# Second MLP in groups of 1024 tokens with seven block products per 2x2 product, the weight sums streamed from memory

## The chip, the cores and the metric

The kernel runs on one core of one Trainium2 chip. The metric is the device time of one execution in microseconds (us). TensorE (PE) multiplies, VectorE (DVE), ScalarE (ACT) and GpSimd (POOL) work on tiles elementwise, and SyncE (SP) issues the transfers between memory and the core's buffers (SBUF). TensorE adds its products up in eight banks of 128x512 float32 (PSUM).

## What is computed

An attention stage yields x, in 8 sequences of 576 tokens with 512 features; two MLP stages follow, the second of which the change touches:

```python
def _moe_ref(x, w_ch1, w_ch2):           # first MLP
    u = x + np.real(fft(fft(x, axis=1), axis=2))
    un = (u - mu) / np.sqrt(var + 1e-06)
    ch = np.maximum(un @ w_ch1, 0.0) @ w_ch2
    return u + ch

def _moe2_ref(x, U, V, w_ch1, w_ch2):    # second MLP
    h = x.transpose(0, 2, 1) @ U @ V
    u = x + h.transpose(0, 2, 1)
    ch = np.maximum(u @ w_ch1, 0.0) @ w_ch2
    return u + ch
```

In both MLPs w_ch1 is 512x2048 and w_ch2 2048x512. All of it is float32, 4608 tokens in all.

## The kernel before

Each MLP runs over NB = 9 blocks of BT = 512 tokens, and in each block over NF = 16 slices of 128 hidden features: 144 passes n for the first MLP (blocks 0 to 8) and 144 for the second (blocks 9 to 17). One loop emits them all. Matrix products take the format fp32r, in which a float32 number is split into a rounded high part and a low part (the difference). Each product is made of three: low times high, high times low, high times high, added up in one bank.

A pass n does the following. `split_w2` and `split_w1` (for two passes ahead) split the slices of the weights: ScalarE rounds (L185, L193), GpSimd or VectorE subtracts (L186, L194). `emit_l1` multiplies the slice of layer one with the block's inputs `xh`, `xl`, 12 products of 128x512 (L208 to L210) into a bank `h`; ScalarE takes relu and rounds into `gh` (L213), VectorE makes the low part `gl` (L214). `emit_l2` of the pass before then adds 12 products into four banks `acc` (L228 to L230 in the first MLP, L232 to L234 in the second). So TensorE has 24 products in a pass, and 384 in a block. After a block's last pass `finish_b` adds u from `t_xsum` (GpSimd, L674) to the four banks and stores the result (L680, L681).

Beside the passes, the table `side[n]` lists what is emitted after pass n: tasks of attention, and `prep_b(j)` for the second MLP, which loads tokens (`t_x2`, L612), splits them (`t_xs`, L625), projects them with U into `pt` (`t_pt`, L635, ten products per sequence) and builds the inputs in transposed form, tile `u` in the trace (`t_u2`, L661 with V, four transposes at L664; then `xh`, `xl`, L666 and L667). The weights of the second MLP are converted during the first by `w_pre` and kept in memory in `wb_d`; `w_get` loads them during block 8. The pool `wpool` then holds all 32 tiles of 128x512.

Order: no scheduler moves anything (`manual_schedule`); on each engine the instructions stand as the code emits them, and each queue, SP's with the transfers too, works strictly in that order. An instruction that waits holds up all behind it on its engine.

## Time and profile before

| | |
|---|---|
| median of 3 runs | 1880.99 us (1880.36 to 1881.33) |
| span of the profiled execution | 1881.6 us; its time outside the profiler is not listed apart |
| TensorE, products / weight loads | busy 1803.6 / 1502.3 us |
| VectorE, ScalarE, GpSimd | busy 953.9, 760.9, 682.0 us |
| second MLP | from 1049.8 us on, some 92.5 us a block |

The profile lists one execution on the chip: the busy time of each engine, groups of equal instructions by line (L12 is line 12 of the kernel), what released an idle engine, and the chain of work that ended last. Products overlap in the records: one of 128x512 is marked busy for some 0.39 us, although the next starts sooner, so the distance of the starts tells the rate. PEld are the weight loads that go with each product.

### The profile page before, as it was taken

How to read it: one execution, taken by the hardware profiler on the slowest of the kernel's cores; microseconds unless marked ns; L12 is line 12 of the kernel's file. 1: busy time of each engine (PE TensorE's matmuls, PEld its weight loads, DVE VectorE, ACT ScalarE, POOL GpSimd, SP SyncE). 2: the span in 40 equal slices, each digit the busy share in tenths (PEclk: the TensorE clock that was granted, in tenths of full speed). 3: DMA queues.
4: the chain of work that ended last, by engine and by line, in shares of the span. 5: the costliest groups of instructions: out<-in, count | busy, mean ns of one | idle time of the engine just before them, and what ended most of it. 6: DMA issues, size and time to landing. Idle time of an engine off the chain costs nothing.

```text
span 1881.6 us, 22636 instructions
## 1 busy us (share of the span) xinstructions
PE 1803.6 (96%) x8520; PEld 1502.3 (80%) x8520; DVE 953.9 (51%) x1494; ACT 760.9 (40%) x1448; POOL 682.0 (36%) x544
## 2 busy tenths in 40 slices
PE   5679999999999999999999999999999999999998
PEld 4557778788887878878888888888888888888887
DVE  6688865858677585845343333333333333333232
ACT  4565343434444343433443333334434343333332
POOL 2456444454534445442222222222222223232322
PEclk8889999999999999999999999999999999999999
DMA  6635324251432425003133101010101010100000
GB/s 249 235 104 205 123 96 147 74 180 57 147 129 97 146 77 177 34 26 86 56 124 111 63 0 51 1 45 1 51 1 45 1 51 1 45 1 23 1 23 23
DMA packets 61517, 146.16 MB, mean 78 GB/s; under 512 B 11144, under 2 KB 13720, under 8 KB 58400
## 3 DMA queue, kind: packets, MB, share of 16 engines
q1 hardware_dynamic: 61408, 144.72, 22.1%
q8 instruction: 67, 1.10, 0.3%
q14 instruction: 42, 0.34, 0.1%
HBM read 106.91 MB, written 39.43 MB: 78 GB/s over the span
## 4 chain that ended last, share of the span: by engine, by line
PE 80%; DVE 11%; ACT 3%; DMA 2%; POOL 1%; issue 1%; SPq 0%; POOLq 0%; ACTq 0%; DVEq 0%
PE h L208 12%; PE h L210 12%; PE h L209 12%; PE acc L234 7%; PE acc L232 7%; PE acc L233 7%; PE acc L228 5%; PE acc L230 5%; PE acc L229 5%; DVE f L333 2%; DMA raw<-in_w2a 2%; DVE eh L362 1%; PE o L294 1%; PE kv L273 1%; DVE f L328 1%
## 5 line engine op out<-in xcount | busy, mean ns | idle before, releaser
L186 POOL TENSOR_TENSOR w1l<-w,w1h 128x512 fp32r<-128x512 f32 x276 | 360.4, 1306 | 959.4 <-ACT w1h L185 959.3
L214 DVE SCALAR_TENSOR_TENSOR gl<-h,gh 128x512 fp32r<-128x512 f32 x288 | 198.3, 689 | 396.7 <-ACT gh L213 396.5
L213 ACT ACTIVATE gh<-h 128x512 fp32r<-128x512 f32 x288 | 171.7, 596 | 500.3 <-PE h L210 498.1
L194 DVE TENSOR_TENSOR w2l<-w,w2h 128x512 fp32r<-128x512 f32 x272 | 214.7, 789 | 179.3 <-ACT w2h L193 178.6
L228 PE MATMUL acc<-w2h,gl 128*128 128x512 f32 x576 | 231.9, 403 | 29.4 <-DVE gl L214 29.2
L193 ACT ACTIVATE w2h<-w 128x512 fp32r<-128x512 f32 x288 | 180.8, 628 | 159.8 <-PE acc L234 111.5
L229 PE MATMUL acc<-w2l,gh 128*128 128x512 f32 x576 | 229.6, 399 | 8.2 <-POOL w2l L194 8.2
L208 PE MATMUL h<-xl,w1h 128*128 128x512 f32 x576 | 228.5, 397 | 1.4 <-DVE xl L531 1.4
L230 PE MATMUL acc<-w2h,gh 128*128 128x512 f32 x576 | 228.9, 397 | 0.0
L208 PE MATMUL h<-xlb,w1h 128*128 128x512 f32 x576 | 227.5, 395 | 0.0
L210 PE MATMUL h<-xhb,w1l 128*128 128x512 f32 x576 | 225.3, 391 | 0.0
L210 PE MATMUL h<-xh,w1l 128*128 128x512 f32 x576 | 225.2, 391 | 0.0
L209 PE MATMUL h<-xh,w1h 128*128 128x512 f32 x576 | 225.1, 391 | 0.0
L209 PE MATMUL h<-xhb,w1h 128*128 128x512 f32 x576 | 224.9, 390 | 0.0
L234 PE MATMUL acc<-gh,w2h 128*128 128x512 f32 x576 | 224.8, 390 | 0.0
L232 PE MATMUL acc<-gh,w2l 128*128 128x512 f32 x576 | 224.2, 389 | 0.0
L233 PE MATMUL acc<-gl,w2h 128*128 128x512 f32 x576 | 224.1, 389 | 0.0
L185 ACT ACTIVATE w1h<-w 128x512 fp32r<-128x512 f32 x288 | 179.9, 625 | 15.1 <-DVE w L116 15.1
L228 PEld LDWEIGHTS acc<-w2h,gl 128*128 128x128 f32 x576 | 110.3, 192 | 59.8 <-DVE gl L214 34.5
L229 PEld LDWEIGHTS acc<-w2l,gh 128*128 128x128 f32 x576 | 110.5, 192 | 33.0 <-POOL w2l L194 10.9
L230 PEld LDWEIGHTS acc<-w2h,gh 128*128 128x128 f32 x576 | 110.8, 192 | 23.4
L210 PEld LDWEIGHTS h<-xh,w1l 128*128 128x128 f32 x576 | 108.3, 188 | 23.9
(137 smaller groups left out, 2642.3 us busy)
## 6 DMA issues: line engine op xcount, KB each, us to landing
kv<-in_kvm SPq DMA_DIRECT2D x14, 1280.0 KB, 9.5
q<-in_qT SPq DMA_DIRECT2D x8, 1220.0 KB, 9.2
x_d<-x2o SPq DMA_DIRECT2D x36, 256.0 KB, 2.1
x2f<-x_d SPq DMA_DIRECT2D x36, 256.0 KB, 4.2
outT<-o SPq DMA_DIRECT2D x36, 256.0 KB, 2.1
u_d<-x SPq DMA_DIRECT2D x32, 256.0 KB, 2.4
raw<-in_w1b SPq DMA_DIRECT2D x16, 512.0 KB
raw<-in_w2b SPq DMA_DIRECT2D x16, 512.0 KB, 4.7
```

Of the source, the lines that this page charges most:

```text
L186: (nc.vector if n in on_dve else nc.gpsimd).tensor_tensor(out=al, in0=a, in1=f32(ah), op=ALU.subtract)
L194: (nc.gpsimd if n in CLP else nc.vector).tensor_tensor(out=cl, in0=c, in1=f32(ch), op=ALU.subtract)
L208: nc.tensor.matmul(out=h, lhsT=ah[:, kc, :], rhs=xl[:, kc, :], start=(kc == 0), stop=False)
L209: nc.tensor.matmul(out=h, lhsT=ah[:, kc, :], rhs=xh[:, kc, :], start=False, stop=False)
L210: nc.tensor.matmul(out=h, lhsT=al[:, kc, :], rhs=xh[:, kc, :], start=False, stop=(kc == 3))
L214: nc.vector.scalar_tensor_tensor(out=gl, in0=h, scalar=0.0, in1=f32(gh), op0=ALU.max, op1=ALU.subtract)
L228: nc.tensor.matmul(out=a, lhsT=gl[:, tt], rhs=ch, start=s, stop=False)
L229: nc.tensor.matmul(out=a, lhsT=gh[:, tt], rhs=cl, start=False, stop=False)
L230: nc.tensor.matmul(out=a, lhsT=gh[:, tt], rhs=ch, start=False, stop=e)
L232: nc.tensor.matmul(out=a, lhsT=cl[:, tt], rhs=gh, start=s, stop=False)
L233: nc.tensor.matmul(out=a, lhsT=ch[:, tt], rhs=gl, start=False, stop=False)
L234: nc.tensor.matmul(out=a, lhsT=ch[:, tt], rhs=gh, start=False, stop=e)
```

## The change

Block 0 of the second MLP (passes 144 to 159) stays. The other eight blocks become four groups of two blocks, `group(1)` to `group(4)`, after the loop. In a group each layer is a product of matrices cut into 2x2 blocks, with seven block products in place of eight by the Strassen-Winograd scheme: four sums of blocks on the side of the weights, four on the side of the inputs, and sums of the products afterwards.

- **Units.** A layer has 56 units, seven products p for each of eight row blocks (m in layer one, i in layer two), of six matrix products of 128x512 each. `P1` runs skewed over m, so that products of neighbouring m alternate; `P2` runs one p over all i. Layer one stands wholly ahead of layer two, its results `G[m]`, four tiles of 128x512, in the buffers that held the weights.
- **Layer one.** Products 0, 4, 5 and 2 of an m add up in one bank `y`, 3 and 6 in `zz`, 1 in `z` (an `h` bank). After each product `post1` copies or adds the partial sum out, on ScalarE or VectorE.
- **Layer two.** `make` splits the input of each unit five units (`LEAD`) ahead, a rounding on ScalarE and a subtraction on VectorE, into six buffers. `plan` spreads over the units the sums T1, T2, T4 of `G`, the output sums F (`o_add`) and, for the next group, the input sums S, roundings H and low parts L (`x_sum`, `x_hi`, `x_lo`). `t_u2` of the next group runs in units 1 to 8 and stores u in memory (`ub_d`); `o_load` loads it again for the output.
- **Weights.** The seven weight blocks of each row block, split into high and low part, are made once by 16 `job`s in four steps a pass apart, two passes from job to job, and stored in `wv_d` (2 x 56 tiles of 256 KB). In the groups `v_load` streams them back, 512 KB for two units, four pairs ahead, into five buffers `v`.
- `split_w1`, `split_w2` and GpSimd have no work in the groups.

```diff
+    def u_copy(j, dc, ps):
+        half, k = divmod(dc, 2)
+        q = (0, 1, 5, 6)[half if j % 2 else 2 + half]
...
+        nc.scalar.activation(out=xb[q, k], in_=ps, func=AF.Copy)
+        nc.sync.dma_start(out=ub_d[j - 1][128 * dc:128 * dc + 128, :], in_=xb[q, k])
...
+    def x_tmp(q, k):
+        xb[q, k], where = x2_tile(f"xb{q}_{k}")
+        x2_held.append(where)
+    def x_sum(p, k):
+        b11, b21, t3, b22 = (xb[q, k] for q in (0, 1, 5, 6))
+        if p == 5:
+            nc.vector.tensor_tensor(out=t3, in0=b22, in1=t3, op=ALU.subtract)
+            return
+        if p == 2:
+            xb[2, k] = b21
+        else:
+            x_tmp(p, k)
+        if p == 4:
+            nc.vector.tensor_tensor(out=xb[4, k], in0=t3, in1=b11, op=ALU.add)
+        else:
+            nc.vector.tensor_tensor(out=xb[p, k], in0=b22 if p == 3 else b21, in1=xb[4, k], op=ALU.subtract)
+    def x_hi(p, k):
+        nc.scalar.activation(out=x_var(p)[1][:, k], in_=xb[p, k], func=AF.Copy)
+    def x_lo(p, k):
+        lo, hi = x_var(p)
+        nc.vector.tensor_tensor(out=lo[:, k], in0=xb[p, k], in1=f32(hi[:, k]), op=ALU.subtract)
...
+    P1 = [(p, r - d) for r in range(9) for p, d in ((0, 0), (2, 1), (1, 0), (6, 1), (4, 0), (3, 0), (5, 0))
+          if 0 <= r - d < 8]
+    P2 = [(p, i) for p in (0, 1, 4, 6, 5, 3, 2) for i in range(8)]
+    LEAD = 5
+    LAST = (NB - 1) // 2
...
+    def job(k, where):
...
+        def load():
...
+            for q in range(2):
+                nc.sync.dma_start(out=t[q], in_=wb_d[2 * NF + 4 * m + 2 * q + ph])
...
+        def first():
+            a11, a12, a21, a22 = r["a"]
+            s1, s2, s3, s4 = (cut(r["s"][q // 2][:, 256 * (q % 2):256 * (q % 2) + 256]) for q in range(4))
+            o = r["o"] = outs(0)
+            for q, v in enumerate((a11, a12, a22)):
+                nc.scalar.activation(out=cut(o[q // 2][:, q % 2, 0]), in_=v, func=AF.Copy)
+            for d, x, y, op in ((s1, a21, a22, ALU.add), (s2, s1, a11, ALU.subtract), (s3, a11, a21, ALU.subtract),
+                                (s4, a12, s2, ALU.subtract)):
+                nc.vector.tensor_tensor(out=d, in0=x, in1=y, op=op)
+        def second():
+            o = r["o"]
+            for q, v in enumerate((r["a"][0], r["a"][1], r["a"][3])):
+                nc.vector.tensor_tensor(out=cut(o[q // 2][:, q % 2, 1]), in0=v, in1=f32(cut(o[q // 2][:, q % 2, 0])),
+                                        op=ALU.subtract)
+            store(o, (0, 1, 2))
+            o = r["o"] = outs(1)
+            for q in range(2):
+                nc.scalar.activation(out=o[q][:, :, 0], in_=cut(r["s"][q]), func=AF.Copy)
+        def third():
+            o = r["o"]
+            for q in range(2):
+                nc.vector.tensor_tensor(out=o[q][:, :, 1], in0=cut(r["s"][q]), in1=f32(o[q][:, :, 0]), op=ALU.subtract)
+            store(o, (3, 4, 5, 6))
...
+    def v_load(c):
+        if c >= 56 * LAST:
+            return
+        ph, k = divmod(c % 56, 28)
+        t = vq[c] = pbx["pb"].tile([128, 2, 2, 256], F32R, tag="v", name=f"v{c}", bufs=5)
+        nc.sync.dma_start(out=f32(t.rearrange("p e h n -> p (e h n)")), in_=wv_d[ph][:, 1024 * k:1024 * k + 1024])
+    def v_unit(g, ph, u):
+        c, e = divmod(112 * (g - 1) + 56 * ph + u, 2)
+        t = vq[c] if e == 0 else vq.pop(c)
+        if e == 0:
+            v_load(c + 4)
+        return t[:, e, 0], t[:, e, 1]
...
+        def post1(p, m):
+            g11, g12, g21, g22 = G[m]
+            if p == 0:
+                act(g11, Y[m], AF.Copy)
+            elif p == 1:
+                tt(g11, Z[m], g11, ALU.add)
+            elif p == 4:
+                act(g12, Y[m], AF.Copy)
+            elif p == 5:
+                act(g22, Y[m], AF.Copy)
+                tt(g22, ZZ[m], g22, ALU.add)
+            elif p == 2:
+                act(g21, Y[m], AF.Relu)
+            elif p == 6:
+                tt(g12, ZZ[m], g12, ALU.add)
+                u = P1.index((p, m))
+                late.setdefault(u + 1, []).append(lambda: act(g12, g12, AF.Relu))
+                late.setdefault(u + 3, []).append(lambda: stt(g12, g22, g12, ALU.subtract))
+        def make(u):
+            p, i = P2[u]
+            src = G[i][{0: 0, 1: 2, 4: 0, 6: 3, 5: 1, 3: 3, 2: 2}[p]]
+            pool, a, b = ((wsp, "w1h", "w1l"), (wsp, "w2h", "w2l"), (gpool, "gh", "gl"))[u % 3]
+            hi, lo = (pool.tile([128, BT], F32R, tag=t, name=f"{t}g{g}_{u}", bufs=2) for t in (a, b))
+            act(hi, src, AF.Relu if p in (0, 6) else AF.Copy)
+            (stt if p in (0, 6) else tt)(lo, src, f32(hi), ALU.subtract)
+            gv[u] = hi, lo
+        for u, (p, m) in enumerate(P1):
...
+            dst = {1: Z, 3: ZZ, 6: ZZ}.get(p, Y)[m]
+            hi, lo = v_unit(g, 0, u)
+            xl, xh = x_var(p)
+            for k in range(2):
+                c = slice(128 * k, 128 * k + 128)
+                for n, (w, r) in enumerate(((hi, xl), (hi, xh), (lo, xh))):
+                    nc.tensor.matmul(out=dst, lhsT=w[:, c], rhs=r[:, k], start=p in (0, 1, 3) and k + n == 0,
+                                     stop=k == 1 and n == 2, skip_group_check=True)
+            post1(p, m)
+            for f in late.pop(u, []) + side1[u]:
+                f()
+            if u + LEAD >= 56:
+                make(u + LEAD - 56)
...
+        def o_add(c, mp, banks, end=False):
+            def f():
+                t = o[c, mp]
+                tt(t, banks[mp], t, ALU.add)
+                if end:
+                    e, j = 2 * mp + c // 2, j1 + c % 2
+                    nc.sync.dma_start(out=outT[128 * e:128 * e + 128, BT * j:BT * j + BT], in_=t)
+            return f
+        ops = {}
+        for i in range(8):
+            g11, g12, g21, g22 = G[i]
+            ops["T2", i] = ("D", max(0, i - 3) if i < 7 else 5, 10 + i, [],
+                            lambda a=g11, b=g12: stt(a, a, b, ALU.add))
+            ops["T1", i] = ("D", 21 + i, 34 + i, [], lambda a=g22, b=g11: stt(a, a, b, ALU.subtract))
+            ops["T4", i] = ("D", 6 + i, 42 + i, [(("T2", i), 1)], lambda a=g21, b=g11: tt(a, a, b, ALU.subtract))
+        for mp in range(2):
+            ops["F11", mp] = ("D", 8, 14, [], o_add(0, mp, YY))
+            ops["F11b", mp] = ("D", 16, 26, [], o_add(0, mp, Z1, True))
+            ops["F12", mp] = ("D", 24, 30, [], o_add(1, mp, YY))
...
+        sched = plan(ops, lambda e, t: 2 if e == "D" and 1 <= t <= 8 else 1)
...
+        for u, (p, i) in enumerate(P2):
...
+            dst = {1: Z1, 6: W, 3: Z3}.get(p, YY)
+            hi, lo = v_unit(g, 1, u)
+            gh, gl = gv.pop(u)
+            for mp in range(2):
+                c = slice(128 * mp, 128 * mp + 128)
+                for n, (w, r) in enumerate(((lo, gh), (hi, gl), (hi, gh))):
+                    nc.tensor.matmul(out=dst[mp], lhsT=w[:, c], rhs=r, start=p in (0, 1, 6, 3) and i + n == 0,
+                                     stop=i == 7 and n == 2, skip_group_check=True)
+            if u + LEAD < 56:
+                make(u + LEAD)
+            for f in late.pop(56 + u, []) + side2.get(u, []):
+                f()
+        for mp in range(2):
+            o_add(2, mp, YY, True)()
...
+        for e in range(4):
+            side[NA + 11 + e].append(lambda e=e: t_xsum(NB, e))
+        place(prep_b(0), NA - NF)
+        starts = [7 * NF + k for k in (5, 7, 9, 14)] + [8 * NF + k for k in (1, 3, 5, 7, 9, 11, 13, 15)] + \
+                 [NA + k for k in (1, 3, 5, 7)]
+        for k, n in enumerate(starts):
+            for d, f in enumerate(job(k, ("x0", "x1", "x2", "o")[k % 4] if k < 8 else ("x2", "o")[k % 2])):
+                side[n + d].append(f)
...
+        for c in range(4):
+            side[NA + 12 + c].append(lambda c=c: v_load(c))
...
-        for n in range(2 * NA):
+        NP = NA + NF
+        for n in range(NP):
...
-        finish(2 * NA - 1, (2, 3))
+        finish(NP - 1, (2, 3))
+        for g in range(1, 5):
+            group(g)
```

How the instructions stand now. First TensorE, at the end of a group's layer one; before, in a pass of the second MLP (names: bank <- operands; x5 are five equal rows; in brackets the engines waited for):

```order
L210 MATMUL h162_9784<-xhb1_9453,w1l162_9722 128x512
L232 MATMUL acc10_0_9754<-gh161_9746,w2l161_9730 128x512 [waits DVE_49,Activation_49]
L233 MATMUL acc10_0_9754<-gl161_9747,w2h161_9729 128x512 [waits DVE_49]
L234 MATMUL acc10_0_9754<-gh161_9746,w2h161_9729 128x512
L232 MATMUL acc10_1_9755<-gh161_9746,w2l161_9730 128x512
```

After, the last round of layer one in group 1 (`xv0` to `xv6` are the inputs of product 0 to 6, `v` the weights):

```order
L953 MATMUL y7_1_10838<-xv4_10189,v25_10779 128x512 [waits Activation_49]
L953 MATMUL y7_1_10838<-xv4_10189,v25_10779 128x512 x5
L953 MATMUL zz7_1_10884<-xv3_10274,v26_10801 128x512 [waits DMAHW2_49]
L953 MATMUL zz7_1_10884<-xv3_10274,v26_10801 128x512 x5
L953 MATMUL y7_1_10838<-xv5_10145,v26_10801 128x512 [waits Activation_49]
L953 MATMUL y7_1_10838<-xv5_10145,v26_10801 128x512 x5
L953 MATMUL y7_1_10838<-xv2_10279,v27_10818 128x512 [waits DMAHW3_49,Activation_49]
L953 MATMUL y7_1_10838<-xv2_10279,v27_10818 128x512 x5
```

Products 5 and 2 of m=7 stand next to each other in one bank, the second waiting for ScalarE; for smaller m a unit of another m stands between them.

Second VectorE, in a pass of the second MLP before:

```order
L194 TENSOR_TENSOR w2l164_9859<-w1_1_4_8517,w2h164_9858 128x512 [waits Activation_49]
L214 SCALAR_TENSOR_TENSOR gl164_9876<-h164_9862,gh164_9875 128x512 [waits Activation_49]
L625 TENSOR_TENSOR x2s2_1_9899<-x2f10_9772,x2s2_1_9899 128x512 [waits Activation_49]
L194 TENSOR_TENSOR w2l165_9903<-w1_1_5_8564,w2h165_9902 128x512 [waits Activation_49]
L214 SCALAR_TENSOR_TENSOR gl165_9920<-h165_9906,gh165_9919 128x512 [waits Activation_49]
```

After, at the start of layer two of group 1 (`w1l`, `w2l`, `gl` with `g1_6` and the like: the low part for unit 6; `g1_3_0`: tile 0 of `G[3]`):

```order
L887 SCALAR_TENSOR_TENSOR w1lg1_6_10957<-g1_6_0_10751,w1hg1_6_10956 128x512 [waits Activation_49]
L887 SCALAR_TENSOR_TENSOR g1_1_0_10359<-g1_1_0_10359,g1_1_1_10360 128x512 [waits DVE_49]
L887 SCALAR_TENSOR_TENSOR g1_2_0_10431<-g1_2_0_10431,g1_2_1_10432 128x512 [waits DVE_49]
L887 SCALAR_TENSOR_TENSOR w2lg1_7_10985<-g1_7_0_10834,w2hg1_7_10984 128x512 [waits PE_49,Activation_49]
L887 SCALAR_TENSOR_TENSOR g1_7_1_10835<-g1_7_3_10837,g1_7_1_10835 128x512
L887 SCALAR_TENSOR_TENSOR g1_3_0_10517<-g1_3_0_10517,g1_3_1_10518 128x512 [waits DVE_49]
L887 SCALAR_TENSOR_TENSOR g1_4_0_10593<-g1_4_0_10593,g1_4_1_10594 128x512 [waits DVE_49]
L884 TENSOR_TENSOR glg1_8_11007<-g1_0_2_10309,ghg1_8_11006 128x512 [waits PE_49,Activation_49]
```

Where two or three operations stood in a pass of 24 products, two sums now stand between the low parts of two neighbouring units of six.

Third SP, in the second MLP before:

```order
L681 DMA outT<-o11_3_11030 128x512 [waits DMAHW2_49,DVE_49]
L612 DMA x2f18_11155<-x2_d4_96 128x512 [waits DMAHW3_49,PE_49,Activation_49]
L612 DMA x2f19_11157<-x2_d4_96 128x512 [waits DMAHW4_49,PE_49,Activation_49]
L612 DMA x2f20_11159<-x2_d5_97 128x512 [waits DMAHW5_49,PE_49,Activation_49]
L612 DMA x2f21_11161<-x2_d5_97 128x512 [waits DMAHW6_49,PE_49,Activation_49]
```

After, from unit 1 of layer two of group 1:

```order
L714 DMA ub_d3_138<-ub3_0_10967 128x512 [waits Activation_49]
L970 DMA o1_0_0_10972<-ub_d1_136 128x512
L970 DMA o1_0_1_10974<-ub_d1_136 128x512
L843 DMA v33_10976<-wv_d1_135 128x1024 [waits DMAHW4_49,PE_49]
L714 DMA ub_d3_138<-ub3_0_10967 128x512 [waits DMAHW5_49,Activation_49]
L714 DMA ub_d3_138<-ub3_1_11017 128x512 [waits DMAHW6_49,Activation_49]
L843 DMA v34_11022<-wv_d1_135 128x1024 [waits DMAHW7_49,PE_49]
L714 DMA ub_d3_138<-ub3_1_11017 128x512 [waits DMAHW0_49,Activation_49]
```

A load of weights now stands behind every one or two stores and loads of u.

## Rows read from the trace of the kernel before

**Rows 1.** The page: span, and busy us (share of the span) x instructions.

```profile
span 1881.6 us, 22636 instructions
PE 1803.6 (96%) x8520; PEld 1502.3 (80%) x8520; DVE 953.9 (51%) x1494; ACT 760.9 (40%) x1448; POOL 682.0 (36%) x544
```

**Rows 2.** Busy time by stretch, two blocks of the second MLP.

```profile
core 0: us, PE busy (x) PEld busy (x) DVE busy (x) ACT busy (x) POOL busy (x), PEclk, DMA share, GB/s
1143.90:1236.50 92.60, 92.60 (x419) 76.77 (x418) 31.24 (x47) 36.56 (x63) 25.71 (x20) 1.00 0.08 26
1236.50:1329.00 92.50, 92.50 (x419) 76.76 (x418) 31.93 (x47) 35.83 (x62) 25.72 (x20) 1.00 0.07 23
```

**Rows 3.** The chain of waits at the end: start us, us, engine and line.

```profile
1852.01 0.23 PE h L208
...
1857.45 0.23 PE h L208
...
1874.23 0.24 PE acc L234
1874.55 0.64 DVE o L680
...
1876.59 0.69 DVE o L680
```

**Rows 4.** Groups from 1200 to 1800 us: busy us, mean ns | idle before.

```profile
L208 PE MATMUL h<-xlb,w1h 128*128 128x512 f32 x417 | 165.0, 396 | 0.0
L234 PE MATMUL acc<-gh,w2h 128*128 128x512 f32 x416 | 162.3, 390 | 0.0
```

**Rows 5.** Timeline from 1500 us: start us, us, engine, line [idle before <-releaser].

```profile
1500.58 0.60 ACT L666 ACTIVATE xhb<-u 128x512 fp32r<-128x512 f32 x1 [2.31 <-PE u L664]
1501.07 0.62 ACT L193 ACTIVATE w2h<-w 128x512 fp32r<-128x512 f32 x1
1501.21 0.69 DVE L667 TENSOR_TENSOR xlb<-u,xhb 128x512 fp32r<-128x512 f32 x1 [2.74 <-ACT xhb L666]
1501.81 0.68 DVE L194 TENSOR_TENSOR w2l<-w,w2h 128x512 fp32r<-128x512 f32 x1
1502.92 0.39 PE L210 MATMUL h<-xhb,w1l 128*128 128x512 f32 x1
1503.34 0.60 ACT L213 ACTIVATE gh<-h 128x512 fp32r<-128x512 f32 x1 [1.65 <-PE h L210]
1503.97 0.69 DVE L214 SCALAR_TENSOR_TENSOR gl<-h,gh 128x512 fp32r<-128x512 f32 x1 [1.48 <-ACT gh L213]
```

**Rows 6.** Busy time by stretch in the opening, columns as in rows 2.

```profile
5.00:10.00 5.00, 3.15 (x15) 3.18 (x16) 0.00 (x0) 0.00 (x0) 0.00 (x0) 1.00 1.11 363
10.00:15.00 5.00, 4.76 (x34) 4.57 (x34) 0.59 (x2) 0.54 (x2) 0.00 (x0) 1.00 1.26 518
...
20.00:25.00 5.00, 0.00 (x0) 0.00 (x0) 4.77 (x12) 2.09 (x9) 5.00 (x4) 0.70 1.02 388
25.00:30.00 5.00, 1.06 (x3) 0.74 (x3) 4.52 (x9) 1.89 (x6) 0.87 (x1) 0.50 1.03 428
```

**Rows 7.** Transfers: xcount, KB each, median us from issue to landing.

```profile
x2f<-x_d SPq DMA_DIRECT2D x36, 256.0 KB, 4.2
...
raw<-in_w2b SPq DMA_DIRECT2D x16, 512.0 KB, 4.7
...
w<-wb_d SPq DMA_DIRECT2D x32, 256.0 KB, 2.9
```

**Rows 8.** Timeline of SP's queue at 98 us, one issue.

```profile
98.87 0.33 SPq L88 DMA_DIRECT2D more_raw<-in_w1a  x1
```

**Rows 9.** Timeline at 1439 us, VectorE and GpSimd.

```profile
1439.16 1.29 POOL L186 TENSOR_TENSOR w1l<-w,w1h 128x512 fp32r<-128x512 f32 x1 [4.14 <-ACT w1h L185]
1439.63 1.37 DVE L625 TENSOR_TENSOR x2s<-x2f,x2s 128x512 fp32r<-128x512 f32 x1 [0.34 <-ACT x2s L624]
```

**Rows 10.** The page's groups, whole run: busy us, mean ns | idle before, releaser.

```profile
L194 DVE TENSOR_TENSOR w2l<-w,w2h 128x512 fp32r<-128x512 f32 x272 | 214.7, 789 | 179.3 <-ACT w2h L193 178.6
```

More of the change, by code (lines that the diff above doesn't have):

```diff
@@ L74 @@
     mu_d = dram.tile([B, S], F32, tag="mu_d", name="mu_d")
+    wv_d = [dram.tile([128, 56 * 512], F32, tag=f"wv_d{k}", name=f"wv_d{k}") for k in range(2)]
+    ub_d = [dram.tile([DM, BT], F32, tag=f"ub_d{j}", name=f"ub_d{j}") for j in range(1, NB)]
     ident = com.tile([128, 128], F32, name="ident")
@@ L578, in x_new @@
     def x_new(j):
[L579 to L581 removed]
+        t = [pbx["pb"].tile([128, 4, BT], F32R, tag=f"x{k}", name=f"{nm}b{j}") for k, nm in enumerate(("xh", "xl"))]
+        return tuple(t)
     def t_b_tables(step):
@@ new lines, in t_u2, with x_var @@
+        if dc == 3:
+            for t in range(4):
+                x2_free.append(x2_at[4 * j + t])
+    XTAG = ((0, "xh"), (0, "xl"), (1, "x2"), (1, "x0"), (0, "res"), (0, "un"), (1, "x1"))
+    xv = {}
+    xb = {}
+    x2_held = []
+    def x_var(p):
+        if p not in xv:
+            k, tag = XTAG[p]
+            t = (pbx["pb"] if k else pa).tile([128, 4, BT], F32R, tag=tag, name=f"xv{p}")
+            xv[p] = t[:, 0:2], t[:, 2:4]
+        return xv[p]
+    def u_copy(j, dc, ps):
+        half, k = divmod(dc, 2)
+        q = (0, 1, 5, 6)[half if j % 2 else 2 + half]
+        if j % 2 and dc == 0:
+            xv.clear()
+            xb.clear()
+        if q < 2:
+            if k == 0:
+                xb[q, "t"] = cvp.tile([128, 2, BT], F32, tag="raw", name=f"ub{j}_{q}", bufs=2)
+            xb[q, k] = xb[q, "t"][:, k]
+        else:
+            x_tmp(q, k)
+        nc.scalar.activation(out=xb[q, k], in_=ps, func=AF.Copy)
+        nc.sync.dma_start(out=ub_d[j - 1][128 * dc:128 * dc + 128, :], in_=xb[q, k])
@@ new lines, in plan @@
+    def plan(ops, cap):
+        at, out, t = {}, {}, 0
+        todo = dict(ops)
+        while todo:
+            for eng in "DA":
+                for _ in range(cap(eng, t)):
+                    ready = [nm for nm, (e, first, last, deps, f) in todo.items() if e == eng and first <= t
+                             and all(d in at and at[d] + lag <= t for d, lag in deps)]
+                    if not ready:
+                        break
+                    nm = min(ready, key=lambda v: todo[v][2])
+                    assert t <= todo[nm][2], (nm, t, todo[nm][2])
+                    at[nm] = t
+                    out.setdefault(t, []).append(todo.pop(nm)[4])
+            t += 1
+            assert t < 200, list(todo)
+        return out
@@ L699 @@
     NA = NB * NF
-    side = {n: [] for n in range(-NF, 2 * NA)}
+    side = {n: [] for n in range(-NF, NA + NF)}
     CONV = 13
```

187 lines of the change are left out of this document (157 added, 30 removed).

## The prediction

> **What bounds the kernel now.** I read the busy shares first [rows 1], then the stretches of the second MLP [rows 2], then the end of the chain of waits [rows 3], then the groups of instructions [rows 4]. TensorE is busy 92.60 of 92.60 us in a block of 512 tokens, at full granted clock, while VectorE has 31.24, ScalarE 36.56 and GpSimd 25.71 us of work [rows 2]. That an engine is marked busy does not yet make it the bound; the chain does: its last 25 us go from one product to the next in steps of 0.23 us, and nothing but VectorE's last four additions stands behind them [rows 3]. Between 1852.01 and 1857.45 lie one pass of layer one and one of layer two, 24 products of 128x512, so one costs 5.44/24 = **0.2267 us**. A block has 16 x 24 = 384 of them, 87.05 us; the other 5.5 us of its 92.6 are the ten products of `pt` (10 x 0.2267 = 2.3) and the four `u` tiles (3.2). Idle time ahead of the products is 0.0 [rows 4]. So a product taken out of this stage is worth its 0.2267 us, as long as all that feeds the others keeps pace.
>
> **What is removed.** Block 0 of the second MLP stays as it is. Blocks 1 to 8 become four groups of two. Two blocks had 2 x 384 = 768 products; a group has 56 units of 6 in each layer, 2 x 56 x 6 = 672. That is 96 fewer per group, 384 in all (the built program falls from 8200 matrix instructions to 7816, so the change does what it says): 384 x 0.2267 = **-87.1 us**. `pt`, `u` and the transposes stay, inside a group. A group then takes 2 x 92.55 - 21.8 = 163.3 us: layer one 76.2 and 20 products of `pt`, 80.7 us; layer two 76.2 and eight `u` tiles, 82.7 us. Gone too are the two roundings per pass (L185, L193) with their subtractions, which hid beside TensorE and so give nothing.
>
> **What is added, and what hides it.**
>
> VectorE and ScalarE, layer two. Per group VectorE gets 56 low parts (`make`), 24 block sums (T1, T2, T4), 14 output sums (F), 8 sums and 14 low parts of the next group's inputs: 116 operations of 128x512. One takes 0.69 us, but the next starts 0.60 us after it (1501.21 to 1501.81 in [rows 5]). That is 70 us by the spacing and 80 us by the duration, against 82.7 us of TensorE: hidden by either, but thinly. The densest place is units 1 to 8 (second order listing): about 20 operations, at most 13.8 us, against 8 x 1.36 us and 6.4 us of `u` tiles. Each low part is made five units, 6.8 us, ahead of its product, which absorbs a burst. ScalarE has 56 + 14 + 8 = 78 copies of 0.60 to 0.63 us, 48 us of 82.7. Layer one is light: 45 operations on VectorE, some 31 of 80.7 us. GpSimd has nothing left to do in the groups, so its subtractions no longer stand in VectorE's way. Cost 0; the other end is a rival below.
>
> One wait is new in each group. In layer one the products 0, 4, 5 and 2 of a row block m add into the same bank, and each sum is copied out before the next may be added. There is always a unit of another m between them, except in the last round: there product 2 of m=7 follows product 5 at once (first order listing). Its first matmul waits for the copy of product 5: a matmul ends 0.39 us after its start, ScalarE starts 0.03 us later and takes 0.60 [rows 5], with 0.03 back that is 1.05 us where 0.227 would do: 0.82 us, **+3.3 us** in four groups.
>
> The weight stream. Every unit needs 256 KB of split weight sums, a pair of units one load of 512 KB in 2.72 us, 193 GB/s; in layer two the stored and reloaded `u` and the outputs (24 x 256 KB) come on top: 21.0 MB in 82.7 us, 254 GB/s, and 4.7 MB in the 17.3 us of units 1 to 8, 271 GB/s. The kernel before never asks that much in this stage (26 GB/s, [rows 2]), so I bound it from the opening, where loads queue up: 363, 518, 388 and 428 GB/s in stretches of 5 us [rows 6]. The demand is half to three quarters of that. A load is issued as soon as the tile four pairs ahead falls free, about 10 us before its use; single loads land in 2.9 us, pairs and more in 4.2 to 4.7 [rows 7]. On SP these loads stand between stores that wait for ScalarE and VectorE (third order listing); with an issue of 0.33 us [rows 8], 5 us are left for such waits. Cost 0.
>
> The sixteen jobs that split the weight sums, two passes apart, in blocks 7 and 8 of the first MLP and block 0 of the second. A job has seven subtractions of 128x256 and two of 128x512 on VectorE, at most 9 x 0.69 = 6.2 us beside 4 x 0.69 = 2.8 us of regular work in two passes of 5.44 us: it fits in 10.9 us, with 1.9 to spare. Its two loads stand on SP behind three stores of the job before, which wait for VectorE; 5 issues x 0.33 and 2.9 to 4.2 us to land make 4.6 to 5.9 us against one pass of 5.44. So a job's first operation can hold VectorE up by half a microsecond or more, and behind it stands the low part `gl` that TensorE needs one pass later. Bounds: 0, if that pass covers it, and a full microsecond in each of the sixteen, 16 us. The first is nearer, since the slack of a pass is over 4 us; I take **+5 us**.
>
> The last five passes of block 0 (27.2 us) also make the first group's inputs: 18 operations and 10 regular ones on VectorE, 28 x 0.69 = 19.3 us. GpSimd has seven operations there, and a VectorE operation with both inputs in SBUF that began 0.47 us into one took 1.37 in place of 0.69 us [rows 9]. Seven times 0.68 make 24.1 us of 27.2: cost 0. The Trainium skill's page "SBUF — State Buffer" (SBUF: two separate sides) says that the two engines share a port pair as an exclusive lock, held for the whole instruction, which the row agrees with. Were each of the seven to hold VectorE for a whole GpSimd operation of 1.29 us, this stretch would have 28.3 us, and a term of +1.1 us would join the sum, which otherwise has none for it.
>
> **Sum.** -87.1 + 3.3 + 5 = -78.8 us. Against the profiled span of 1881.6 us that is 1802.8; the median of the runs lies 0.6 us under the span, so **1802 us**. At the end nothing changes: two additions and their stores after the last product, four before, as in [rows 3].
>
> **Rivals.**
>
> *VectorE falls behind in layer two.* For it: 116 operations in 82.7 us leave little, and nearly each low part first waits for a ScalarE copy, which opens gaps that the spacing of 0.60 us doesn't have. Against: its cover of five units, and GpSimd's silence. If an operation costs 0.79 us (L194's mean over the whole run, [rows 10], with waits for the port in it), 116 take 91.6 us, 8.9 over; the lead hides up to 6.8 us of that or, if each layer starts without one, none: 2 to 9 us in three groups, while the last has only 94 operations. Time 1808 to 1829 us.
>
> *The jobs cost their full price*, +16 in place of +5, because each waits for its loads with the next low part behind it: 1813 us.
>
> *The weight stream sets the pace*: slower than before. Place: every unit of the four groups, which waits for its tile `v`. A group moves 38.0 MB (56 x 512 KB, 24 x 256 KB, nine inputs of 256 KB). Before, its two blocks took 185.1 us, so the stream must sustain 38.0/185.1 = **205 GB/s**; under that the kernel is slower, and the waits would also let the granted clock fall (0.50 and 0.70 where TensorE idles in the opening, [rows 6]). At 190 GB/s a group takes 200 us, 37 more than forecast, and the whole 1802 + 4 x 37 = 1950 us. For it: the tiles are cut from rows 112 KB apart, which no transfer of the kernel before does; if loads ran one after another, 512 KB in 4.7 us would be 112 GB/s. Against: the opening's 363 to 518 GB/s were made of loads of this size and more from the same queue.
>
> *All is hidden*: -87.1 or, with the short pauses of the old passes gone as well, up to -89: 1792 us.
>
> **How the numbers follow.** Forecast as summed, between all hidden and the dearer jobs (1791 to 1815): 0.70. VectorE late, or it and the jobs, 1815 to 1834: 0.13. A larger part of the gain lost, 1834 to 1877: 0.08. The stream under 205 GB/s: 0.06. A gain eaten up to within 0.2% (3.8 us, about what a measurement of this kernel can tell from no change): 0.02. Under 1791: 0.01. The range of eight in ten takes the first case and most of the second, **1791 to 1834**. Faster 0.92, same 0.02, slower 0.06.
>
> **What would show it.** In the changed profile a group should take about 164 us; products should be 0.227 us apart; in each group one wait of 0.8 us for a copy of `y` by ScalarE; VectorE busy 75 to 95% in layer two with few waits of TensorE on it; `v` loads landing in 3 to 5 us with no wait of TensorE for a DMA; waits of some microseconds in all in the stretch from 910 to 1145 us. Waits of TensorE on `v`, a granted clock below 1.00 in the groups, or layer two much longer than 83 us would prove me wrong.

## The result and the profile after

The changed kernel takes 1822.52 us (median of four runs, 1822.16 to 1824.96) where the kernel before took 1881.16 in the same comparison: a ratio of 0.9689, 95% interval 0.9675 to 0.9702, or 58.6 us less. Forecast were 1802 us and a range of 1791 to 1834. So the direction and the range hold, but 20.5 us of the expected gain of 79 are missing. They are the subject of what follows.

The head of the page of the profiled run, which answers to [rows 1] (span, then busy us, share of the span and instructions of each engine):

```profile
span 1820.5 us, 22972 instructions
PE 1737.2 (95%) x8136; PEld 1432.6 (79%) x8136; DVE 1191.6 (65%) x1918; ACT 830.0 (46%) x1584; POOL 478.7 (26%) x384
```

TensorE has 384 instructions fewer (8520 to 8136), as the change says, but only 66.4 us less busy time, not 87. The stretches of the four groups, layer by layer, answer to [rows 2] (columns as there; shown are group 1 and group 4):

```profile
core 0: us, PE busy (x) PEld busy (x) DVE busy (x) ACT busy (x) POOL busy (x), PEclk, DMA share, GB/s
1157.65:1241.46 83.81, 83.12 (x357) 66.79 (x356) 33.20 (x52) 37.65 (x65) 0.00 (x0) 1.00 0.69 215
1241.46:1325.38 83.92, 83.92 (x385) 68.61 (x384) 72.93 (x115) 44.31 (x75) 0.00 (x0) 1.00 0.74 237
...
1658.96:1738.10 79.14, 78.45 (x337) 62.98 (x336) 23.68 (x36) 24.85 (x44) 0.00 (x0) 1.00 0.67 201
1738.10:1816.28 78.18, 78.18 (x337) 62.89 (x335) 59.45 (x94) 33.20 (x54) 0.00 (x0) 1.00 0.66 209
```

TensorE is busy for the whole of layer two at the full granted clock, and VectorE for 87% of it, without TensorE waiting for it. Yet layer two of group 4, 336 products and nothing else, takes 78.4 us to the end of its last product's slot, not the 76.2 that 336 x 0.2267 make. The chain of waits at the end (start us, us, engine and line; x48 are 48 products that follow each other without a gap) says the same, where [rows 3] had 24 products in 5.44 us:

```profile
1749.48 11.20 PE z L1033 x48
1760.68 11.20 PE yy L1033 x48
```

11.20/48 = **0.2333 us** from product to product. That spacing, not a wait, is the largest thing that the prediction did not have.

The waits of TensorE are those that were named: four for a copy of `y`, 0.7 us each, and none in the groups beside them. This is the complete list for the groups (1157 to 1817 us):

```profile
PE y L953 <- ACT g L890: 2.7, 4, 0.7
```

The weight stream never held TensorE up: 224 loads of 512 KB landed in 4.0 us (median from issue to landing, [rows 7] had 2.9 to 4.7), and layer two moved 237 GB/s.

```profile
v<-wv_d SPq DMA_DIRECT2D x224, 512.0 KB, 4.0
...
job<-wb_d SPq DMA_DIRECT2D x32, 256.0 KB, 3.4
```

In the stage of the sixteen jobs (900 to 1160 us) TensorE waited, in four lines of the list (us in total, times, longest):

```profile
PE pt L649 <- DVE x2s L639: 3.3, 1, 3.3
PE acc L230 <- DVE gl L216: 2.8, 2, 1.8
PE acc L234 <- DVE x2o L546: 1.1, 1, 1.1
PE u L671 <- DVE pts L656: 0.7, 1, 0.7
```

With the start of the pipeline after each, six gaps of 8.9 us in all. The longest, at 1077 us, in the timelines of SP and of VectorE (start us, us, engine, line, [idle before <- releaser]):

```profile
1066.44 1.55 SPq L831 DMA_DIRECT2D wv_d<-vo  x3
1068.05 1.81 SPq L792 DMA_DIRECT2D job<-wb_d  x2
```

```profile
1074.37 1.55 DVE L811 TENSOR_TENSOR job<-job 128x256 f32<-128x256 f32 x4 [4.64 <-DMA job<-wb_d]
1076.33 0.69 DVE L639 TENSOR_TENSOR x2s<-x2f,x2s 128x512 fp32r<-128x512 f32 x1 [0.40 <-ACT x2s L638]
```

The job's two loads are issued by 1069.86, behind four loads of `x`, one of weights and three stores; VectorE idles 4.64 us until they are there, and `x2s`, which TensorE needs next, stands behind the job on ScalarE and VectorE.

Put together, span against span (1820.5 against 1881.6). In the kernel before, blocks 1 to 8 ran from 1143.85 to the start of the last product at 1876.10 us, 732.2 us; the 5.5 us of `pt` and `u` of one block, which now run in block 0, and 87.05 us of products less make 639.7. The groups ran from 1157.65 to 1816.28, 658.6 us. The shares of the difference come from the experiments below. The row of the short pauses is a remainder that no run isolates; it agrees with the starts of the products, which lie 228.2 ns apart on average in blocks 1 to 8 of the kernel before and 227.7 in the groups of `all_fix`.

| term | predicted | measured | from |
|---|---|---|---|
| 384 products fewer | -87.1 | -87.1 | count x 0.2267 |
| spacing of the other products in the groups | 0 | +16.6 | groups 658.6, with equal offsets 642.0 |
| wait for the copy of `y` | +3.3 | +3.9 | groups 642.0, without it 638.1 |
| short pauses of the old passes | 0 | -1.6 | 638.1 against 639.7 |
| all up to the first group | +5 | +8.3 | 1157.65 against 1143.85 + 5.5 |
| the end behind the last product | 0 | -1.3 | 4.2 us against 5.5 |
| sum | -78.8 | -61.2 | spans: -61.1 |

The other 2.8 us of the miss lie outside the span: the median is 2.0 us above the profiled span, while the forecast lay 0.8 below its own.

### The profile page after: what moved, and what is told of

The parts are those of the page before. It is cut to its first block, busy times and chain, and to the rows that moved or that the text cites. A ratio compares the mean times of both kernels' runs of the same rounds, so it can differ in the third digit from the quotient of the medians.

```text
span 1820.5 us, 22972 instructions
## 1 busy us (share of the span) xinstructions
PE 1737.2 (95%) x8136; PEld 1432.6 (79%) x8136; DVE 1191.6 (65%) x1918; ACT 830.0 (46%) x1584; POOL 478.7 (26%) x384
## 4 chain that ended last, share of the span: by engine, by line
PE 76%; DVE 12%; ACT 4%; DMA 3%; issue 2%; POOL 2%; SPq 1%; ACTq 0%; POOLq 0%; DVEq 0%
PE y L953 10%; PE yy L1033 10%; PE h L210 5%; PE h L212 5%; PE h L211 5%; PE acc L230 5%; PE acc L232 5%; PE z L1033 5%; PE acc L231 5%; PE zz L953 5%; PE z L953 2%; PE w L1033 2%; DVE f L335 2%; PE o L296 2%; DVE eh L364 2%
## 5 line engine op out<-in xcount | busy, mean ns | idle before, releaser
L188 POOL TENSOR_TENSOR w1l<-w,w1h 128x512 fp32r<-128x512 f32 x148 | 196.0, 1325 | 445.6 <-ACT w1h L187 422.2
L210 PE MATMUL h<-xl,w1h 128*128 128x512 f32 x576 | 229.1, 398 | 1.4 <-DVE xl L533 1.4
L953 PE MATMUL y<-xv,v 128*128 128x512 f32 x768 | 192.2, 396 | 2.7 <-ACT g L890 2.7
L215 ACT ACTIVATE gh<-h 128x512 fp32r<-128x512 f32 x160 | 94.5, 591 | 179.6 <-PE h L212 177.3
L953 PEld LDWEIGHTS y<-xv,v 128*128 128x128 f32 x768 | 143.9, 188 | 38.9 <-ACT g L890 4.5
L216 DVE SCALAR_TENSOR_TENSOR gl<-h,gh 128x512 fp32r<-128x512 f32 x160 | 109.6, 686 | 98.8 <-ACT gh L215 98.5
L196 DVE TENSOR_TENSOR w2l<-w,w2h 128x512 fp32r<-128x512 f32 x144 | 126.3, 877 | 48.9 <-ACT w2h L195 48.4
L210 PEld LDWEIGHTS h<-xl,w1h 128*128 128x128 f32 x576 | 108.8, 189 | 22.7 <-DVE xl L533 1.8
L211 PEld LDWEIGHTS h<-xh,w1h 128*128 128x128 f32 x576 | 108.7, 189 | 20.9
L195 ACT ACTIVATE w2h<-w 128x512 fp32r<-128x512 f32 x160 | 99.8, 624 | 38.9 <-PE acc L232 35.3
L187 ACT ACTIVATE w1h<-w 128x512 fp32r<-128x512 f32 x160 | 99.7, 623 | 14.7 <-DVE w L118 14.7
```

Of the source, the lines that this page charges most:

```text
L188: (nc.vector if n in on_dve else nc.gpsimd).tensor_tensor(out=al, in0=a, in1=f32(ah), op=ALU.subtract)
L195: nc.scalar.activation(out=ch, in_=c, func=AF.Copy)
L196: (nc.gpsimd if n in CLP else nc.vector).tensor_tensor(out=cl, in0=c, in1=f32(ch), op=ALU.subtract)
L210: nc.tensor.matmul(out=h, lhsT=ah[:, kc, :], rhs=xl[:, kc, :], start=(kc == 0), stop=False)
L211: nc.tensor.matmul(out=h, lhsT=ah[:, kc, :], rhs=xh[:, kc, :], start=False, stop=False)
L216: nc.vector.scalar_tensor_tensor(out=gl, in0=h, scalar=0.0, in1=f32(gh), op0=ALU.max, op1=ALU.subtract)
```

## Experiments: why the products came at 0.2333 us

**Height, and transfers.** The new products differ from the old in three ways that no instruction count shows: their weights `v` come by a stream of loads, the tiles lie elsewhere in SBUF, and the units write and add in a new pattern of banks. In layer one of block 0, whose code did not change and whose input tiles all lie in the upper pool, the spacing was high too (234 ns), which spoke for the place.

`low_pb` moves the pool down without touching an instruction (pools with `side="right"` are laid out from the top of SBUF):

```
-    wpool = ctx.enter_context(tc.tile_pool(name="wpool", bufs=NF))
-    cvp = ctx.enter_context(tc.tile_pool(name="cvp", bufs=1))
+    wpool = ctx.enter_context(tc.tile_pool(name="wpool", bufs=NF, side="right"))
+    cvp = ctx.enter_context(tc.tile_pool(name="cvp", bufs=1, side="right"))
```

> The changed kernel with one thing moved: the pools of the weights in original form and of the scratch tiles are taken from the top of SBUF, so that the pool that holds the split weight sums `v`, three of the seven input sums and the inputs of block 0 lies at 64 to 148 KB of each partition in place of 140 to 224 KB. Not one instruction is added, removed or reordered. Theory 'place': a product whose stationary or moving operand lies high in SBUF while the other lies low starts 233 ns after the one before it, and 227 ns if both lie low. Then the products of the four groups come 0.2267 us apart, a layer without side work takes 336 x 0.2267 = 76.2 us (it took 78.4 to 79.1), and the whole is 1822.5 - 16 (groups) - 1.3 (layer one of block 0) = 1805 us. Rival 'transfers': the stream of 512 KB loads into SBUF slows the reads of TensorE; then nothing changes, 1822 us. Rival 'order': the sequence of banks and waits in the new units costs it; again 1822 us.

It took 1824.38 us (ratio 0.9699, 0.9677 to 0.9722); the groups took 658.6 us, as in the changed kernel to a tenth. This move in height changes nothing.

`no_stream` drops the loads:

```
+        if c >= 5:
+            vq[c] = v_kept[c % 5]
+            return
-        t = vq[c] = pbx["pb"].tile([128, 2, 2, 256], F32R, tag="v", name=f"v{c}", bufs=5)
+        t = vq[c] = v_kept[c] = pbx["pb"].tile([128, 2, 2, 256], F32R, tag="v", name=f"v{c}", bufs=5)
```

> The changed kernel without the stream of weight sums: only the first five loads of `v` are made, and all later units use these five tiles over and over, so its output is not that of the reference. Layout and order stay. Theory 'place': products stay 0.233 us apart, 1822 us within 2 (the loads were hidden). Rival 'transfers': 0.2267 us, 1806 us. Rival 'the stream's waits': if some wait for a load cost time that the profile puts elsewhere, some us less at an unchanged cadence.

1824.85 us. Layer two of group 1 (columns as in [rows 2]):

```profile
1243.25:1327.17 83.92, 83.92 (x385) 68.60 (x384) 72.98 (x115) 44.37 (x75) 0.00 (x0) 1.00 0.20 70
```

70 in place of 237 GB/s, and 83.92 us as with the stream. Transfers cost these products nothing, and no wait for them was hidden elsewhere. The Trainium skill says on its page "SBUF — State Buffer" (Who interferes with whom) that DMA never contends with a compute engine; by that rule this run had to come out as it did, and it agrees: 83.92 us at either rate.

`wsp_high` is the kernel before with its split weights moved away (`side="right"` on the pool `wsp`):

> The kernel before with one pool moved: the split weights w1h, w1l, w2h, w2l (16 KB, stationary in layer one of both MLPs and in layer two of the second, moving in layer two of the first) go from 4 to 20 KB of a partition to the top of SBUF. No instruction changes. Theory 'place': nearly all of the 6912 large products then read one operand high and one low, 233 in place of 227.5 ns: 6912 x 5.8 ns = +40 us, 1921 us. Rivals 'transfers' and 'order': 1881 us as before.

1914.71 us, ratio 1.0175 (1.0155 to 1.0196). A stretch of one block, which took 92.60 us in [rows 2], with the same counts on the other engines:

```profile
1157.94:1252.72 94.78, 94.78 (x420) 76.77 (x419) 31.23 (x47) 36.54 (x63) 25.59 (x20) 1.00 0.07 26
```

So placement alone does make every product slower (2.2 us on 384, 5.7 ns each), without any transfer or new unit. What it is in the placement, the run leaves open.

**A boundary at 64 KB.** The next theory was that both operands must lie under 64 KB, which all fast products so far did.

`v_low` puts `v` there; its core:

```
-    XTAG = ((0, "xh"), (0, "xl"), (1, "x2"), (1, "x0"), (0, "res"), (0, "un"), (1, "x1"))
+    XTAG = ((0, "xh"), (0, "xl"), (1, "x2"), (1, "x0"), (1, "xa"), (1, "xb"), (1, "x1"))
...
-        t = vq[c] = pbx["pb"].tile([128, 2, 2, 256], F32R, tag="v", name=f"v{c}", bufs=5)
+        t = vq[c] = pa.tile([128, 2, 2, 256], F32R, tag=("un0", "un1", "res0", "res1")[c % 4], name=f"v{c}")
...
-        if e == 0:
-            v_load(c + 4)
+        if e == 0 and c:
+            v_load(c + 3)
```

> The changed kernel with the tiles `v` (four in place of five, loaded three pairs ahead in place of four) in the places of `un` and `res`, at 44 to 60 KB of a partition, and the two input sums that lay there moved up to 165 to 181 KB. In layer two all that TensorE reads then lies under 64 KB (w and g tiles at 4 to 28 KB); in layer one only the input sums 0 and 1 and `v` do. Theory '64 KB' (a product is 227 ns only if both operands lie under 64 KB, about 233 if not): layer two loses 336 x 6.3 ns = 2.1 us in each group, layer one stays about as it was (two sevenths of its products become 227, the rest go from 231 to 233.5 to 234), so 1822.5 - 8.5 = 1814 us. Rival 'something else in the new units' (banks, waits): 1822 us. With a lead of three pairs, 8 us, loads that land in 4 us should still not be waited for.

1816.52 us (ratio 0.9657, 0.9641 to 0.9673). Layer two of the last group fell to 76.2 us, 48 products to 10.88; layer one stayed. No load was waited for with a lead of three pairs.

```profile
1765.34 10.88 PE w L1035 x48
```

That fits the theory, and so does any other in which the old place of `un` and `res` is a good one. `wsp_49` decides between them: the pool `wsp` of the kernel before is opened after `pa`.

> The kernel before with the split weights w1h, w1l, w2h, w2l at 48 to 64 KB of a partition (they were at 4 to 20 KB; at the top of SBUF they made the kernel 33 us slower). Theory '64 KB': nothing changes, 1881 us. Theory 'distance to the other operand' or a boundary further down: in between, up to 1914 us.

1908.74 us, ratio 1.0145 (1.0125 to 1.0165); a block took 94.73 us. All operands of the large products in blocks 1 to 8 lay under 64.1 KB, and the same heights that were fast for `v` in `v_low` were slow here. The theory of a boundary falls.

**Offsets.** What the tiles of these runs have in common shows in the addresses that the built program gives them (they do not stand in the profile). The small tiles ahead of the pools make all tiles of 4 to 61 KB begin 32 bytes past a multiple of 128; the 160 bytes of layer norm tiles behind them shift everything above to 64. In `wsp_high` the weights began at 96, in `wsp_49` at 64, in `v_low` the new place of `v` at 32. With unused tiles, three runs set one offset for both operands of all but four of the 6616 large products; this is `align_32`:

```
         pa.tile([128, 4, BT], F32, tag=t, name="first_" + t)
+    pa.tile([128, 24], F32, tag="pad", name="pad")
```

> The changed kernel with one unused tile of 96 bytes put behind the small tiles of the layer norm, so that all that lies above it moves up by 96 bytes. In the changed kernel all tiles that TensorE reads from 4 to 61 KB begin 32 bytes past a multiple of 128, and those from 131 KB up (`v`, three input sums, the inputs of block 0) 64 past one; in the runs so far a product took 227 to 228 ns where both operands began at 32, and 231 to 234 where one or both began at 64 or 96. The pad brings all to 32. Theory 'alignment': 227 ns everywhere, so the groups lose 2688 x 5.9 ns = 15.9 us and layer one of block 0 loses 1.2: 1805 us. Rival 'height in SBUF' with a boundary that the runs have not shown: nothing moves by more than 96 bytes, 1822 us.

> The changed kernel with two unused tiles of 96 bytes, one at 2 KB and the one of the run above, so that all tiles that TensorE reads in both MLPs begin at a multiple of 128 bytes. Theory 'equal offsets are fast, whatever they are': 227 ns everywhere, 1805 us. Theory 'an offset of 32 is the fast one': the first MLP's products too go from 227.5 to about 231 ns (as the few with both at 64 did), 3456 x 3.5 ns = +12 us there, and the groups stay at 231 to 233: about 1830 us. Theory 'a multiple of 128 is the best': below 1805 us.

> The changed kernel with two unused tiles, of 32 bytes at 2 KB and of 96 bytes behind the layer norm's tiles, so that all tiles that TensorE reads in both MLPs begin 64 bytes past a multiple of 128. With all at 32 it took 1804 us, with all at 0 1802 us. Theory 'equal offsets are fast, whatever they are': again 227 ns everywhere and 1802 to 1804 us. Theory 'an operand that begins at 64 or 96 is slow by itself' (for it: in the changed kernel the products with both operands at 64 took 231 ns, though they stand in units between others with 32 and 64): all 6616 large products, not only those of the groups, take about 231 ns, 6616 x 3.9 ns = +26 us, 1828 to 1830 us.

Measured: 1804.1 (ratio 0.9587, 0.9573 to 0.9602), 1802.2 (0.9577, 0.9561 to 0.9593) and 1801.9 us (0.9591, 0.9575 to 0.9607); the groups took 642.0, 642.1 and 642.0 us. In the chain of `align_32`, `v` at 165 to 185 KB and the stream running:

```profile
1732.56 10.88 PE z L1034 x48
1743.44 10.88 PE yy L1034 x48
```

| kernel, stretch | offset of weights / of inputs, bytes | us per product |
|---|---|---|
| before, second MLP, blocks 1 to 8 | 32 / 32 | 0.2267 |
| before, second MLP, block 0, layer one | 32 / 32, in one product of three 32 / 64 | 0.2327 |
| after and `low_pb`, layer two | 64 / 32 | 0.2333 |
| `v_low`, layer two | 32 / 32 | 0.2267 |
| `wsp_high`, `wsp_49`, second MLP, blocks 1 to 8 | 96 / 32, 64 / 32 | 5.5 to 5.7 ns more than before |
| `align_32`, `align_0`, `align_64`, groups | 32 / 32, 0 / 0, 64 / 64 | 0.2267 |

So what counts is that the two operands of all products in a stream begin at the same offset, not which one it is, nor how high they lie. Equality modulo 64 does not suffice (96 beside 32 is slow); whether the modulus is 128 or 256 these runs don't tell, while tiles that differ by 256 modulo 512 were fast.

A product also owes something to its neighbours. In the changed kernel products with both operands at 64, in units between others at 64 and 32, came 231 ns apart on average. The trace of before has a plainer case: in block 0 the tile `xlb` alone lies in the upper pool, at 64, so only the products of L208 are unequal and those of L209 and L210 are not. From the start of layer one of a pass to that of layer two, twelve products take 2.80 us:

```profile
1063.68 0.40 PE L208 MATMUL h<-xlb,w1h 128*128 128x512 f32 x1
...
1066.48 0.40 PE L232 MATMUL acc<-gh,w2l 128*128 128x512 f32 x1
```

That is 0.2333 us each, and over the whole layer all three lines are slow (231.8, 232.3 and 234.1 ns to the next start). One unequal product in three slowed them all. Why it is so, and how far the effect of a neighbour reaches, stays open.

## Experiments: the other terms

**The wait for `y`.** `last_round` reorders the last nine units:

```
-          if 0 <= r - d < 8]
+          if 0 <= r - d < 8][:-9] + \
+         [(0, 7), (2, 6), (4, 7), (3, 7), (5, 7), (6, 6), (2, 7), (1, 7), (6, 7)]
```

> The changed kernel with only the order of the last nine units of layer one altered (0/7, 2/6, 4/7, 3/7, 5/7, 6/6, 2/7, 1/7, 6/7 as product/row block), so that between two products into the bank of `y7` there is always another unit. The profile of the changed kernel shows four waits of 0.7 us there. Theory 'that wait is all': -2.7 to -3.0 us, 1819.7 us, and no wait of TensorE on a copy of `y`. Rival 'it comes back' (the sum of `zz` or a low part is late instead): 1822 us with waits of the same size on VectorE.

1819.78 us. The ratio, 0.9672 (0.9658 to 0.9687), overlaps that of the changed kernel, but the trace decides: no wait of TensorE is left in the groups, and they take 654.9 in place of 658.6 us, a stretch that `low_pb`, `no_stream` and `job_early` repeat to 0.1 us. The wait cost 0.9 us in each group, and nothing took its place.

**The jobs.** `job_early` issues a job's loads a pass sooner:

```
-                side[n + d].append(f)
+                side[n + d - (d == 0)].append(f)
```

> The changed kernel with the loads of each of the sixteen jobs issued one pass (5.4 us) earlier, two passes ahead of their use. The changed kernel loses about 8.9 us in six waits of TensorE between 909 and 1157 us; ahead of them VectorE and ScalarE wait up to 6.8 us for a job's loads, which stand on SP behind stores and loads of x. Theory 'loads late': most of that goes, 1822.5 - 6 to 8 = 1815 to 1816 us. Rival 'VectorE and ScalarE are simply full there': at most 2 us go, 1821 us.

1818.63 us (0.9667, 0.9653 to 0.9681), 3.9 less. Not all of that is the edit's: in the profiled run the first group starts 3.8 us earlier (1153.89 against 1157.65), but 1.1 us of it stands already at the first product of pass 116 (884.95 against 886.09), ahead of the first load that was moved. The edit brought 2.6 us, between the 2 of the rival and the 6 to 8 that were expected of the loads. VectorE no longer waits for `job`, but between 1040 and 1110 us these stand in the list of waits:

```profile
ACT vo L808 <- DMA wv_d<-vo: 9.2, 2, 5.7
...
PE pt L649 <- DVE x2s L639: 3.4, 2, 2.5
```

ScalarE now waits for a tile `vo` whose store has not ended (five tiles, four to a job), and `x2s` is queued behind that copy as it was behind the loads. The late loads were the first limit of a job, its five output tiles the second.

**VectorE's room.** `low_twice` repeats one line of `make`:

```
-            (stt if p in (0, 6) else tt)(lo, src, f32(hi), ALU.subtract)
+            for _ in range(2):
+                (stt if p in (0, 6) else tt)(lo, src, f32(hi), ALU.subtract)
```

> The changed kernel with every low part of layer two's activations written twice by VectorE (56 operations of 128x512 more per group, same values). It measures how far VectorE is from being the bound there, and which price of an operation counts. Layer two then has 116 + 56 = 172 operations on VectorE (150 in the last group). By the duration of 0.69 us: 119 us (104) against 84 (78), so 3 x 35 + 25 = +130 us, 1952 us. By the spacing of 0.60 us: 103 us (90), 3 x 19 + 12 = +69 us, 1892 us. If VectorE had room to spare as the wait list says (no wait of TensorE for a low part), the time rises less than either only if an operation costs under 0.49 us: 172 x 0.49 = 84 us.

1913.58 us, between the two prices. Layer two of the first and of the last group:

```profile
1241.28:1346.46 105.18, 94.82 (x385) 65.44 (x384) 103.34 (x165) 42.28 (x75) 0.00 (x0) 1.00 0.54 172
1806.35:1901.30 94.95, 85.00 (x337) 61.02 (x336) 93.11 (x147) 33.06 (x53) 0.00 (x0) 1.00 0.52 161
```

VectorE is full here (103.34 of 105.18 us). The stretch holds 165 operations, since the first low parts are made in layer one; that is 0.64 us each (147 in 94.95: 0.65). Their starts show two prices: each of the 53 repeats, which writes a tile again at once, begins 0.71 to 0.72 us after the operation before it, and all others **0.60 to 0.61 us** after it. For the kernel's own operations that is the spacing, not the duration of 0.69. Of the 88.7 us by which the span grew, 80 lie in the four layers two, 5.6 in layer one, where the first low parts are made, and 3.7 behind the last product. At 0.61 the 116 operations of the changed kernel need 71 of 84 us: the rival "VectorE falls behind" was some 13 us a group away, and is ruled out.

**Together.** `all_fix` has the pad of `align_32`, the order of `last_round`, the loads of `job_early` and, as a fourth edit, the loads of `x` for blocks 1 and 2 a pass earlier:

```
-            side[NA + n].append(lambda b=b: [t_x2(i) for i in x2_first(b)])
+            side[NA - 1 + n].append(lambda b=b: [t_x2(i) for i in x2_first(b)])
```

> The changed kernel with the pad of 96 bytes that brings all tiles to one offset (1804 us alone), the new order of the last nine units of layer one (-2.7 us alone), the loads of the jobs one pass earlier (-3.9 us alone), and the loads of `x` for blocks 1 and 2 one pass earlier too, since in the run with earlier job loads TensorE still waited 3.4 us for `x2s`, made from an `x` that was loaded only one pass before. Theory 'the parts are independent': 1804 - 2.7 - 3.9 - 3 = 1794 us. Rival 'the waits of the stage with the jobs share one cause, VectorE and ScalarE with too much to do': the last term brings nothing, 1797 us.

1798.9 us (five runs, 1795.5 to 1799.6), ratio 0.9565 (0.9552 to 0.9578): the best version here. The groups take 638.1 us, free of waits. The fourth edit brought nothing; its wait moved to the sum of the first MLP's output at the block's border:

```profile
PE acc L234 <- DVE x2o L547: 3.4, 1, 3.4
PE pt L650 <- DVE x2s L640: 1.6, 1, 1.6
PE acc L230 <- DVE gl L216: 1.0, 1, 1.0
PE u L672 <- DVE pts L657: 0.7, 1, 0.7
```

6.7 us, where `job_early` had 5.9. Behind the longest wait, which ended at 1056.02 us, the granted clock fell to 0.50 (1.2 GHz) for 3 us (columns as in [rows 2]):

```profile
1057.40:1060.50 3.10, 3.10 (x9) 2.38 (x8) 3.06 (x8) 1.05 (x2) 0.00 (x0) 0.50 1.04 389
```

Products came 0.427 us apart there, which cost some 1.5 us. The same stands once in the trace of `align_32` (0.51 from 1075.60 to 1079.00) and twice in that of `last_round`, in the stage of the jobs too, and not in those of the changed kernel and of `job_early`. So a wait in this stage can cost more than its length. That VectorE and ScalarE have too much to do in these passes, with the jobs and the inputs of three blocks at once, agrees with it, but no run took work away there, so it is not shown.

## Why the prediction was right, and where it fell short

The range holds in part by luck. The forecast as summed, with its chance of 0.70, ended at 1815 us; the part from 1815 to 1834, where the time lies, was given to VectorE falling behind, alone or with dearer jobs (0.13). VectorE did not fall behind. What brought the time there was the spacing of the products, which no rival named, and of the signs that were to be seen, products 0.227 us apart was the one that failed.

- **What bounds the kernel**: right. The gain came from products taken out, and each was worth its 0.2267 us once the rest was aligned: the groups of `all_fix` take 638.1 us, where the products counted down from the kernel before leave 639.7.
- **The products that remain**: the step that failed. The term of 384 x 0.2267 was sized on the products of before and carried over to new ones, with other tiles. That cost 16.6 us in the groups, by far the most of the miss. In layer one of block 0 (192 products) they came 234.0 ns apart; there the kernel before already had 232.7, so the change lost 0.2 us, not the 1.2 that equal offsets save. No row of before names an offset; what could have warned was at hand, though: in the trace of before layer one of block 0 came 232.7 ns apart where blocks 1 and 2 had 228, the ten `pt` products of a block, whose tiles lie in the upper pool, came 229 to 232 ns apart, and the addresses stand in the built program.
- **One wait in each group**: right in place, cause and size (0.82 us put down, 0.69 listed, 0.92 by the layer's length).
- **VectorE in layer two**: right, and the lower of the two prices was the true one (0.61 us, from `low_twice`). Busy for 72.9 of 83.9 us, no wait of TensorE on it.
- **The weight stream**: right. Loads landed in 4.0 us; the slower rival never came near, as `no_stream` shows.
- **The jobs**: right in mechanism, short in size. Six gaps of 8.9 us stood against a term of 5 that lay between 0 and 16. The prediction counted on a slack of over 4 us in a pass; the wait of VectorE for a load reached 6.8 us, and ScalarE's copies wait with it. In the case shown above loads of `x` stand ahead of the job's on SP, which the prediction did not count. All up to the first group lost 8.3 us: the 8.9, 0.2 for the offsets in block 0, and 1.5 back from an opening that ended sooner in this run, which leaves 0.7 open.
- **The inputs of group 1 in block 0**: right. After a gap at 1111 us TensorE had none up to the first group. The term of +1.1 us, which the prediction worked out from the Trainium skill's rule on the port pair, did not appear.
- **All hidden, and the end**: the remainder of 1.6 us fits the pauses of the old passes, for which the last rival allowed up to 1.9, and the end, put at nothing, gave 1.3. Two additions and stores stand there in place of four, which fits; but of the four in [rows 3] the first began at 1874.55 us, ahead of the last product (1876.10), so they did not all follow it as the prediction has it, and no run tested the cause.

## What to carry to other kernels

A product's price holds for the tiles that it was measured on: before it is carried over to new tiles, compare where their operands begin, and pad so that all that TensorE reads starts at one offset. An unused tile of 96 bytes was worth 18 us here, a third as much as the whole rewrite. When work is inserted into passes, give its loads a lead by what stands ahead of them on the queue, not by a pass, and count its output tiles too.

## What was not expected of the hardware

Products of 128x512 in fp32r came 0.2267 us apart where the tiles of weights and inputs began at the same offset in all products of a stream (0, 32 or 64 bytes past a multiple of 128) and 0.2333 where they began at 64 and 32, at a granted clock of 1.00 in both cases and with nothing waiting; 96 and 32 cost 5.7 ns a product. The Trainium skill's page "SBUF — State Buffer" (Who interferes with whom) gives TensorE two independent read ports, one for the moving operand and one for the weights. By that alone the place of one would not matter to the other; the runs here show that it does, by 2.9% of a product.

On a VectorE that was hardly ever idle (`low_twice`), operations of 128x512 whose records last 0.68 to 0.69 us began 0.60 to 0.61 us apart, and 0.71 to 0.72 where the second wrote the tile that the first had just written.

After an idle stretch of TensorE of 3.4 us its granted clock stood at 0.50 for 3 us in `all_fix` and at 1.00 after one of 3.3 us in the changed kernel, so one length of wait does not have one price.
